# Less scratch for Pool, more tiles in four rings, and a norm moved to the end of a block in a hand-ordered attention and MLP kernel

## The chip, the cores and the metric

The kernel runs on one core of a Trainium2 chip. The metric is the device time of one execution in microseconds, from the start of the program to its end; lower is better.

## The reference

The layer takes x of 2048 rows by 512, computes an attention and a two-layer MLP from it, and mixes both by a gate for each row:

```python
q = (x @ wq).reshape(B, S, 32, 16).transpose(0, 2, 1, 3)
k, v = x @ wk, x @ wv                     # one head of 16 for all 32 query heads
p = softmax(einsum("bhqd,bkd->bhqk", q, k) * 16 ** -0.5)
a = einsum("bhqk,bkd->bhqd", p, v).transpose(0, 2, 1, 3).reshape(B, S, 512) @ wo
h = relu(x @ w1 + b1) ** 2                # 1792 hidden columns
b = h @ w2 + b2
g = sigmoid((x * gate_w).sum(-1, keepdims=True))
return g * a + (1 - g) * b
```

All inputs are float32, and the scores are large (wq and wk are scaled by about 36).

## The kernel before

Rows are worked on in four chunks of 512. Attention goes through 32 *groups* (a chunk and four heads; `it` counts them). A group is 32 *units*: a unit `u` is 128 keys by 256 queries for four heads. For each unit TensorE makes scores, ScalarE takes their exp into a tile `e` of 8 KB for each partition (two units share a tile), and TensorE multiplies the exps with v into `acc`. The second row of `acc` for each value holds the sums that the result is divided by.

A float32 product is made of three products of rounded halves: r and l, where r is the rounded value and l what is left. `split` makes both on VectorE. For weights `w_round` makes r on ScalarE or VectorE and `w_rest` makes l on VectorE. Other work has to be fitted in between: the query products (`q_unit`), the MLP (`hidden` for w1, `summed` for w2) and the output product (`projection`). They come as *spans* of up to 12 pairs of matmuls.

The order of the instructions is written out by hand: nothing is moved later. The main loop alternates two steps:

- `phase` scores some units ahead (`AHEAD` is 4) and places the pairs of a span between them, in an order that `PLANS` gives: M is a pair of the span, S0 the two halves of unit 0's scores in a PSUM tile `s` (two of these exist), and 02 and 12 the halves of unit 2, which go through the single PSUM bank `x` and are copied to `e` by VectorE (`score_copy`, L782).
- `context` multiplies the exps of 6 or 4 older units with v (L812). `block` chooses 6 or 4; a span of 12 is either put in one block of 6 units or halved over two blocks of 4.

While it writes the program, the planner keeps estimated clocks for three engines (`at_pe`, `at_act`, `at_dve`). `spend` fills VectorE's free time before a score copy is due, in this order: the l half of a rounded weight, `soon`, `divisions`, `chores`. A chore may be a load that is queued on SyncE; `held` then keeps the next chore back for some time (6 us by the plan).

`finish` ends a group. ScalarE copies `acc` out (L845), SyncE unpacks it into `oc` (values) and `lc` (sums) with two transfers (L203 and L204, called from `unpack`), and after each second group 24 small operations on VectorE divide (`divide`, L826 to L833); then Pool writes `oc` to the scratch array oTs (L859). When the first group of the next pair ends, a loop empties `divisions` before `oc` and `lc` are taken again. Later `ask` loads oTs into the stage tile (L961) and splits it into `orr` and `orl` (L191, L192) for the output product. `q_load` (L433) loads the queries of the next group with eight transfers.

`qnorm` makes the norms of the queries of a chunk: four small products into `x` (L412), two operations on VectorE (L347, L348), and writes on SyncE. It is called four times in the loop, at the start of a `phase`.

SyncE, ScalarE, VectorE and Pool work in the order of the program: a transfer that waits for its buffer holds all that are queued behind it on the same engine.

The pool `at` has these rings: e with 4 tiles, w1 pairs 3, w2 pairs 4, oc and lc one each. When the last query product is done, a fifth e tile is used as well, in the place of wql (`q_over`). By default 16384 bytes of each partition are set aside for the descriptors of Pool's transfers.

Of the kernel before, what the change touches and what calls it, by code (L numbers as in the profile page):

```python
# [10 lines left out]
F32 = mybir.dt.float32  # L11
# [21 lines left out]
ROOT = float(0x1fbd1df5 + 0x80000)  # L33
WARM = 10
PARTS = [slice(a, min(a + 86, CH)) for a in range(0, CH, 86)]
LANDS, DIVIDES = 6.0, 10.0
PAIR, CONTEXT, TURN, EXP, COPY, LATE = 0.235, 0.429, 0.36, 0.925, 0.66, 0.3
GROUPS = (0, 1, 2, 3), (4, 5, 6, 7), (8, 9, 10), (11, 12, 13)
AHEAD = 4
WHOLE, FIRST, SECOND = range(3)  # L40
PLANS = {
    (6, 12, WHOLE): ("M 02 S0 M S1 M M M M M S3 M M M S4 12 M M S5", (0, 1, 3, 4, 5, 2)),
    (6, 9, WHOLE): ("S0 M 03 M S1 M M M S2 M M M S4 13 M S5", (0, 1, 2, 4, 5, 3)),
    (6, 6, WHOLE): ("S0 M S1 M 03 M S2 M 13 M S4 M S5", (0, 1, 2, 4, 3, 5)),
    (6, 6, SECOND): ("S0 M S1 M 03 M S2 M 13 M S4 M S5", (0, 1, 2, 4, 3, 5)),
# [117 lines left out]
def mix_kernel(ctx: ExitStack, tc: tile.TileContext, xT, wkv, wq, wo, w12, b1, b2, cst, out):  # L163
# [63 lines left out]
    with fast, tc.tile_pool(name="at", bufs=1) as at, \  # L227
# [21 lines left out]
        def x_load(c):  # L249

            if c < 2:
                xw[c] = at.tile([128, KT, CH], F32, name="xf", tag="e", bufs=4)
                for a in range(2):
                    nc.sync.dma_start(xw[c][:, 2 * a:2 * a + 2], xT[c, 2 * a:2 * a + 2].rearrange("k p s -> p k s"))
            for k in range(KT):
                if c < 2:
                    xf[c, k] = xw[c][:, k]
                else:
                    xf[c, k] = at.tile([128, CH], F32, name="xk", tag="w2r" if c == 2 else "w2l", bufs=4)
                    nc.sync.dma_start(xf[c, k], xT[c, k])  # L260

        def wq_load(ts):
# [19 lines left out]

        kvp = [sp.tile([128, 2, CH], F32, name="s") for _ in range(2)]
        ks = {0: kvp[0][:, 0], 1: kvp[0][:, 1], 3: kvp[1][:, 0]}
        sqk = at.tile([96, NC, CH], BF, name="sqk", tag="e", bufs=4)
        kvc = at.tile([128, NC, CH], F32, name="kvc", tag="e", bufs=4)
        kvq, kb = {}, {}

        def kv_half(c, a):
# [153 lines left out]
                staged.append(keep.tile(sh, F32, name="stage", tag="r2"))  # L443
            return staged[0]

        room = [3, 4]
        at_pe, at_act, at_dve = 0.0, 0.0, 0.0

        def act(d, ready=0.0):
# [27 lines left out]
        def w_round(half, copy):  # L477
            n = len(rounded[half])
            assert n < room[half]
            rounded[half][n] = [at.tile([128, 512], F32R, name=f"w{half + 1}{x}", bufs=3 + half) for x in "rl"]  # L480
            copy(rounded[half][n][0], wf[half][n])
            if copy == scalar_copy:
                since[half][n] = act(0.64)
            else:
                since[half][n] = dve(0.46)

# [133 lines left out]
        def spend(until=None):  # L620

            nonlocal held

            def fits(d, ready=0.0):
                return until is None or max(at_dve, ready) + d <= until

            while True:
                due = [i for i in halves() if len(rounded[i]) > len(ws[i])]
                if due and fits(0.68, since[due[0]][len(ws[due[0]])]):
                    w_rest(due[0])  # L630
                elif soon and fits(soon[0][1]):
                    dve(soon[0][1])
                    soon.pop(0)[2]()
                elif divisions and fits(*divisions[0][:2]):
                    d, ready, f = divisions.pop(0)
                    dve(d, ready)
                    f()
                elif chores and fits(chores[0][0], held):
                    d, f = chores.pop(0)
                    dve(d, held if d else 0.0)  # L640
                    if f():
                        held = max(at_dve, at_pe) + 6.0
                else:
                    return

# [46 lines left out]
        def x_again(c):  # L692

            r, l = [xp.tile(sh, F32R, name=f"x{n}again{c}", tag=f"x{n}{c - 2}") for n in "rl"]
            def load(a):
                nc.sync.dma_start(stage()[:, :2], xT[c, 2 * a:2 * a + 2].rearrange("k p s -> p k s"))
                return True

            def part(k):
                split(r[:, k], l[:, k], stage()[:, k % 2])  # L700
                if k == KT - 1:
                    x[c] = r, l

# [36 lines left out]
            return (it, k // 2, k % 2) if it < NC * NG - 1 else (it, k % NK, k // NK)  # L740

        freed, used_x, made = [0.0, 0.0], [0.0], {}
        parts, copied, fifth = {}, {}, [None] * 4

        def e_half(u):

            for t in range(len(es), u // 2 + 1):
                if q_over and len(fifth) % 5 == 4:
                    es[t] = keep.tile([128, 4, CH], F32, name="e5", tag="r1")
                else:  # L750
                    es[t] = at.tile([128, 4, CH], F32, name="e", bufs=4)
                if q_over:
                    fifth.append(None)
            t = u // 2
            return es[t][:, :, u % 2 * HC:u % 2 * HC + HC]

# [44 lines left out]
        def context(acc, us):  # L801

            nonlocal at_pe
            at_pe += 0.12
            while us:
                u, (it, kt, q) = us[0], place(us[0])
                n = 2 if u % 2 == 0 and len(us) > 1 and it < NC * NG - 1 else 1
                at_pe = max([at_pe] + [made[i] + 0.06 for i in us[:n]]) + CONTEXT * n
                us = us[n:]
                cols, mine = slice(q * HC, (q + n) * HC), slice(u % 2 * HC, (u % 2 + n) * HC)  # L810
                for h in range(4):
                    nc.tensor.matmul(acc[h * 32:(h + 1) * 32, cols], v_ext[:, kt],  # L812
                                     es[u // 2][:, h % 2 * 2 + h // 2, mine], start=(kt == 0), stop=(kt == NK - 1),
                                     skip_group_check=True, tile_position=(0, h * 32))
            at_pe += 0.24

        ol = {}
# [17 lines left out]
        def finish(it, acc):  # L835
# [9 lines left out]
            nc.scalar.activation(a, acc, AF.Copy)  # L845
            act(0.62, at_pe)
            if u == 0:
                while divisions:
                    divisions.pop(0)[2]()
                ol[c, t] = [at.tile([128, CH], F32, name=n) for n in ("oc", "lc")]  # L850
            o, l = ol[c, t]
            unpack(nc.sync, o[u * 64:u * 64 + 64], l[u * 64:u * 64 + 64], a)
            if u == 1:
                for q, cols in enumerate(PARTS):
                    i = len(PARTS) * (4 * c + t) + q
                    divisions.extend((d, at_act + DIVIDES, f) for d, f in divide(o, l, cols, ok[:, i:i + 1]))
# [9 lines left out]
        def turn(a, u, js, okc, idle=0):  # L866

            if not o2:
                o2.append(at.tile([128, 4, 2, 4, DH], F32, name="o2", tag="oc"))
            js = slice(js[0], js[-1] + 1)  # L870
            m = js.stop - js.start
            if m > 2:
# [7 lines left out]
            n = at.tile([128, 2, 4, 4], F32, name="nl", bufs=2)[:, :, :m]  # L880
# [9 lines left out]
        def half(acc, q):  # L890

            js = range(2 * q, 2 * q + 2)
            a = at.tile([128, CH], F32, name="ah", tag="accs" if q else "lc")
            nc.vector.tensor_copy(a[:, :HC], acc[:, q * HC:q * HC + HC])
            busy(2 * q)
            if not q:
# [35 lines left out]
        def o_ready(c):  # L932

            if c == 0 and not wos:
                wos.extend(xp.tile(sh, F32R, name=n, tag=t) for n, t in (("wor", "xr2"), ("wol", "xl2")))

                def load(a):
                    nc.sync.dma_start(stage()[:, :2], wo[a * 256:a * 256 + 256].rearrange("(t p) n -> p t n", p=128))
                    return True

                for t in range(KT):
                    if t % 2 == 0:
# [5 lines left out]
        def ask(c, n=KT):  # L948
# [7 lines left out]
            def load(a):  # L956
# [2 lines left out]
                m = min(2, n - 2 * a)  # L959
                i = c * NG + 4 * a  # L960
                nc.sync.dma_start(stage()[:, :m], oTs[i:i + 2 * m].rearrange("(t u) d n -> (u d) t n", u=2))  # L961
                return True

            def part(t):
                orr, orl = tiles
# [9 lines left out]
        def ask_one(c, t):  # L975
# [5 lines left out]
            def load():  # L981
                i = c * NG + 2 * t
                nc.sync.dma_start(stage()[:, :1], oTs[i:i + 2].rearrange("(t u) d n -> (u d) t n", u=2))
                return True

            def part():
                split(osp[c][0][:, t], osp[c][1][:, t], stage()[:, 0])
# [141 lines left out]
        def phase(slots, n, m):  # L1129

            nonlocal scored, evicted, at_pe
            step_aside()
            if narrow:
                used_x[0] = dve(1.3) + 0.06
                qnorm(narrow.pop(0))
            if span.done[0] == 0:
                begin()
            kind = SECOND if span.done[0] else WHOLE if slots == span.slots else FIRST
            text, order = PLANS.get((n, slots, kind)) or plain(n, slots)
            rows = [], []  # L1140
            for item in text.split():
# [40 lines left out]
        def block(u):  # L1182
# [7 lines left out]
                return min(m, rest), left  # L1190
            if span.done[0] == 0 and left > 9:
                halved[0] += max(0.0, (total - 56 - u - 6 * units_left[0]) / (1.6 * max(units_left[0], 1)))
            if rest == 8 or rest == 4 or left > 9 and halved[0] >= 1.0 and rest != 6:
                halved[0] -= 1.0
                return 4, (left + 1) // 2
            return min(rest, 6), left

        halved, units_left = [0.5], [NC * (NF + 16) + 15 + 12]

        acc, us = None, ()  # L1200
        fetch()
# [79 lines left out]
```

## Time and profile before

| | us |
|---|---|
| median of 3 runs | 1242.66 |
| lowest and highest | 1241.65, 1244.49 |
| profiled execution, its own time | 1243.74 |
| its span, first to last instruction | 1242.0 |
| TensorE busy | 1219.7 |
| ScalarE busy | 1038.9 |
| VectorE busy | 767.0 |
| Pool busy | 67.3 |

The mean clock granted to TensorE is 0.992 of full speed. Busy times come from the one profiled execution, which took 1.08 us more than the median. In a row of the profile the engine stands first (PE is TensorE's matmuls, PEld its weight loads, DVE VectorE, ACT ScalarE, SP SyncE), then the line of the kernel and the tiles as out<-in. Matmul ends are modelled, so a busy PE may still be losing some tenths of a microsecond.

### The profile page before, as it was taken

What the parts mean: (1) busy time and instruction counts of PE and PEld (TensorE: products, weight loads), DVE (VectorE), ACT (ScalarE), POOL (GpSimd) and SP (SyncE); (2) the same over time, 40 slices, a digit from 0 to 9 for tenths busy, and PEclk for the clock granted to TensorE, in tenths of its full rate; (3) what the DMA queues carried; (4) which work ended last, traced back from release to release, by engine and by line L of the source; (5) the groups of instructions that cost most, each with busy time, mean ns of one, the idle gap of its engine ahead of it and who ended that gap; (6) DMA issues with size and microseconds to landing.
All of it is one profiled execution on the core that took longest, in us unless ns stands there. A gap on an engine that the chain in (4) does not pass through costs nothing.

```text
span 1242.0 us, 24097 instructions
## 1 busy us (share of the span) xinstructions
PE 1219.7 (98%) x9838; PEld 674.0 (54%) x9839; DVE 767.0 (62%) x1507; ACT 1038.9 (84%) x1151; POOL 67.3 (5%) x87
## 2 busy tenths in 40 slices
PE   9999999999999999999999999999999999999997
PEld 4554555555555545555555556555555555554553
DVE  6765667567485854738477674755838577465543
ACT  6788788888898878888798888888888888887864
POOL 1000120000000110000002001000000000000000
PEclk9999999999999999999999999999999999999989
DMA  6334331211213122102124212112112222300011
GB/s 225 85 106 112 91 94 42 65 57 56 64 61 116 56 82 94 58 21 65 56 82 132 77 41 92 46 48 65 62 67 61 73 65 82 90 31 27 23 51 37
DMA packets 45349, 88.72 MB, mean 71 GB/s; under 512 B 10643, under 2 KB 10899, under 8 KB 44721
## 3 DMA queue, kind: packets, MB, share of 16 engines
q1 hardware_dynamic: 37024, 68.27, 18.2%
q0 software_dynamic: 8064, 18.59, 4.7%
q8 instruction: 79, 1.29, 0.5%
q14 instruction: 38, 0.30, 0.1%
q10 hardware_dynamic: 144, 0.26, 0.1%
HBM read 57.83 MB, written 20.97 MB: 63 GB/s over the span
## 4 chain that ended last, share of the span: by engine, by line
PE 90%; ACT 5%; DVE 2%; DMA 1%; issue 1%; SPq 0%; ACTq 0%; DVEq 0%
PE acc L812 35%; PE mm L1102 31%; PE s L761 16%; PE x L761 5%; ACT e L798 4%; DMA stage<-oTs 1%; PE mm L295 0%; DMA qa<-qs 0%; DVE e L782 0%; PE acc L524 0%; PE mm L199 0%; DVE n L832 0%; ACT w1r L495 0%; DVE tmp L347 0%; SPq L433 0%
## 5 line engine op out<-in xcount | busy, mean ns | idle before, releaser
L798 ACT ACTIVATE e<-s 128x1024 f32<-128x1024 f32 x825 | 786.1, 1025 | 176.8 <-PE s L761 158.7
L812 PE MATMUL acc<-e,v_ext 128*32 128x512 f32 (+1 forms) x4224 | 487.4, 590 | 0.0
L782 DVE COPY e<-x 128x512 f32<-128x512 f32 x398 | 274.6, 690 | 329.2 <-PE x L761 284.5
L761 PE MATMUL s<-qa,k_aug 49*128 49x512 f32 x1650 | 466.4, 414 | 1.8 <-ACT e L798 1.2
L761 PEld LDWEIGHTS s<-qa,k_aug 49*128 49x128 f32 x1650 | 235.8, 185 | 79.5 <-ACT e L798 54.5
L812 PEld LDWEIGHTS acc<-e,v_ext 128*32 128x32 f32 x4224 | 117.2, 110 | 244.6 <-issue 241.3
L1102 PE MATMUL mm<-w2r,hr 64*128 64x512 f32 x896 | 228.5, 402 | 0.0
L798 ACT ACTIVATE e<-e 128x1024 f32<-128x1024 f32 x199 | 211.1, 1061 | 0.4 <-DVE e L782 0.4
L761 PE MATMUL x<-qa,k_aug 49*128 49x512 f32 x398 | 162.9, 409 | 7.8 <-DVE e L782 6.1
L1102 PEld LDWEIGHTS mm<-w2r,hr 64*128 64x128 f32 x896 | 136.0, 186 | 46.3 <-DVE hr L192 15.9
L1102 PE MATMUL mm<-w2l,hr 64*128 64x512 f32 x448 | 144.9, 393 | 0.0
L761 PEld LDWEIGHTS x<-qa,k_aug 49*128 49x128 f32 x398 | 74.3, 187 | 52.2 <-issue 10.9
L1102 PEld LDWEIGHTS mm<-w2l,hr 64*128 64x128 f32 x448 | 80.8, 186 | 6.8
L1102 PE MATMUL mm<-xragain,w1r 64*128 64x512 f32 x224 | 76.8, 418 | 0.2
L1102 PE MATMUL mm<-xr,w1r 64*128 64x512 f32 x224 | 74.1, 417 | 0.3
L1102 PE MATMUL mm<-xlagain,w1r 64*128 64x512 f32 x224 | 74.3, 391 | 0.0
L1102 PE MATMUL mm<-xragain,w1l 64*128 64x512 f32 x224 | 73.3, 392 | 0.0
L1102 PE MATMUL mm<-xl,w1r 64*128 64x512 f32 x224 | 72.4, 392 | 0.0
L1102 PE MATMUL mm<-xr,w1l 64*128 64x512 f32 x224 | 71.4, 393 | 0.0
L832 DVE RECIPROCAL n<-n 128x86 f32<-128x86 f32 x90 | 61.5, 684 | 2.0
L1102 PEld LDWEIGHTS mm<-xragain,w1r 64*128 64x128 f32 x224 | 38.4, 185 | 28.5 <-issue 11.7
L1102 PEld LDWEIGHTS mm<-xr,w1r 64*128 64x128 f32 x224 | 37.5, 185 | 27.5 <-issue 10.4
(162 smaller groups left out, 1178.2 us busy)
## 6 DMA issues: line engine op xcount, KB each, us to landing
stage<-in_w SPq DMA_DIRECT2D x56, 256.0 KB
qa<-qs SPq DMA_DIRECT2D x186, 64.0 KB
w1f<-in_w SPq DMA_DIRECT2D x28, 256.0 KB
w2f<-in_w SPq DMA_DIRECT2D x28, 256.0 KB
qs<-qr SPq DMA_DIRECT2D x16, 256.0 KB
ress<-res POOLq DMA_DIRECT2D x4, 1024.0 KB, 4.9
qs<-ql POOLq DMA_DIRECT2D x15, 256.0 KB, 8.7
oc<-accs SPq DMA_DIRECT2D x30, 128.0 KB
```

The source lines that it names most:

```text
L761: nc.tensor.matmul(dst.rearrange("p (a n) -> p a n", a=2), k_aug[rows, kt * 128:(kt + 1) * 128], qa[it][rows, :, q * HC:q * HC + HC], star ...
L782: nc.vector.tensor_copy(e_half(u)[:, 2 * r:2 * r + 2], x.rearrange("p (a n) -> p a n", a=2))
L798: nc.scalar.activation(e_half(u), src, AF.Exp, scale=SCALE)
L812: nc.tensor.matmul(acc[h * 32:(h + 1) * 32, cols], v_ext[:, kt], es[u // 2][:, h % 2 * 2 + h // 2, mine], start=(kt == 0), stop=(kt == NK ...
L832: return ((0.23, bound), (0.35, compare), (0.72, lambda: nc.vector.reciprocal(n[0], n[0])), (0.28, lambda: nc.vector.tensor_tensor(o[:, co ...
L1102: nc.tensor.matmul((self.before if r else self).bank, a[p], b[p], start=not r and i == 0, stop=r == 1 and i == len(self.terms[1]) - 1, ski ...
```

## The change

The diff makes these edits.

- Pool's descriptor scratch is 1024 bytes instead of 16384. The room goes to a fifth e tile (from the start of the kernel; the one in the place of wql becomes the sixth), a second oc and a second lc tile, and a fifth pair of w2 tiles (`room[1]` is 5).
- The loop that emptied `divisions` when the first group of a pair ends is gone.
- The l half of a weight that ScalarE rounds is planned 0.7 us later (`SURE`).
- A chore that loads returns its own hold: 6 us (`LANDS`) or, for the loads of `ask`, 10 us (`DIVIDES`). The division of the last chunk's third pair is planned 6 us after its copy instead of 10.
- `qnorm` is called at the end of `context` instead of the start of `phase`, and the planner counts its time on TensorE and VectorE. The block after it keeps its 12 slots together and uses the plan `LATER`, in which the first half of unit 2 comes behind S0, S1 and five pairs.
- `block` no longer halves a span when 10 units of a group are left.
- Smaller: the ring of `nl` has one tile, and the tiles that share the rings of oc and lc say bufs=2.

```diff
-LANDS, DIVIDES = 6.0, 10.0
+LANDS, DIVIDES, SURE = 6.0, 10.0, 0.7
-WHOLE, FIRST, SECOND = range(3)
+WHOLE, FIRST, SECOND, LATER = range(4)
 PLANS = {
     (6, 12, WHOLE): ("M 02 S0 M S1 M M M M M S3 M M M S4 12 M M S5", (0, 1, 3, 4, 5, 2)),
+    (6, 12, LATER): ("S0 M M S1 M M M 02 M S3 M M M S4 M 12 M M S5", (0, 1, 3, 4, 5, 2)),
...
-                xw[c] = at.tile([128, KT, CH], F32, name="xf", tag="e", bufs=4)
+                xw[c] = at.tile([128, KT, CH], F32, name="xf", tag="e", bufs=5)
...
-        room = [3, 4]
+        room = [3, 5]
...
-            rounded[half][n] = [at.tile([128, 512], F32R, name=f"w{half + 1}{x}", bufs=3 + half) for x in "rl"]
+            rounded[half][n] = [at.tile([128, 512], F32R, name=f"w{half + 1}{x}", bufs=3 + 2 * half) for x in "rl"]
             copy(rounded[half][n][0], wf[half][n])
             if copy == scalar_copy:
-                since[half][n] = act(0.64)
+                since[half][n] = act(0.64) + SURE
...
                     dve(d, held if d else 0.0)
-                    if f():
-                        held = max(at_dve, at_pe) + 6.0
+                    wait = f()
+                    if wait:
+                        held = max(at_dve, at_pe) + wait
...
-        parts, copied, fifth = {}, {}, [None] * 4
+        parts, copied, sixth = {}, {}, [None] * 5
...
-                if q_over and len(fifth) % 5 == 4:
+                if q_over and len(sixth) % 6 == 5:
                     es[t] = keep.tile([128, 4, CH], F32, name="e5", tag="r1")
                 else:
-                    es[t] = at.tile([128, 4, CH], F32, name="e", bufs=4)
+                    es[t] = at.tile([128, 4, CH], F32, name="e", bufs=5)
...
                                      skip_group_check=True, tile_position=(0, h * 32))
+            if narrow:
+                at_pe = max(at_pe + 0.2, used_x[0] + 0.05)
+                qnorm(narrow.pop(0))
+                late.append(True)
+                used_x[0] = dve(1.3, at_pe + 0.2) + 0.06
             at_pe += 0.24
...
             if u == 0:
-                while divisions:
-                    divisions.pop(0)[2]()
-                ol[c, t] = [at.tile([128, CH], F32, name=n) for n in ("oc", "lc")]
+                ol[c, t] = [at.tile([128, CH], F32, name=n, bufs=2) for n in ("oc", "lc")]
...
-                    divisions.extend((d, at_act + DIVIDES, f) for d, f in divide(o, l, cols, ok[:, i:i + 1]))
+                    divisions.extend((d, at_act + (LANDS if (c, t) == (NC - 1, 2) else DIVIDES), f) for d, f in divide(o, l, cols, ok[:, i:i + 1]))
...
                 nc.sync.dma_start(stage()[:, :m], oTs[i:i + 2 * m].rearrange("(t u) d n -> (u d) t n", u=2))
-                return True
+                return DIVIDES
...
             step_aside()
-            if narrow:
-                used_x[0] = dve(1.3) + 0.06
-                qnorm(narrow.pop(0))
             if span.done[0] == 0:
                 begin()
             kind = SECOND if span.done[0] else WHOLE if slots == span.slots else FIRST
+            if late and (n, slots, kind) == (6, 12, WHOLE):
+                kind = LATER
+            late.clear()
...
-            if rest == 8 or rest == 4 or left > 9 and halved[0] >= 1.0 and rest != 6:
+            if rest == 8 or rest == 4 or left > 9 and halved[0] >= 1.0 and rest not in (6, 10) and not late:
...
-    nc = bacc.Bacc("TRN2", target_bir_lowering=False, num_devices=1)
+    nc = bacc.Bacc("TRN2", target_bir_lowering=False, num_devices=1, dynamic_dma_scratch_size=1024)
```

The lines left out set bufs=5 for the other users of the ring e, bufs=5 for the tiles of x in the rings of w2, `LANDS` as the hold of the other loads, and the ring sizes of nl, o2 and ah.

More of the change, by code (lines that the diff above doesn't have):

```diff
@@ L258, in x_load @@
                 else:
-                    xf[c, k] = at.tile([128, CH], F32, name="xk", tag="w2r" if c == 2 else "w2l", bufs=4)
+                    xf[c, k] = at.tile([128, CH], F32, name="xk", tag="w2r" if c == 2 else "w2l", bufs=5)
                     nc.sync.dma_start(xf[c, k], xT[c, k])
@@ L284, in mix_kernel @@
         ks = {0: kvp[0][:, 0], 1: kvp[0][:, 1], 3: kvp[1][:, 0]}
-        sqk = at.tile([96, NC, CH], BF, name="sqk", tag="e", bufs=4)
-        kvc = at.tile([128, NC, CH], F32, name="kvc", tag="e", bufs=4)
+        sqk = at.tile([96, NC, CH], BF, name="sqk", tag="e", bufs=5)
+        kvc = at.tile([128, NC, CH], F32, name="kvc", tag="e", bufs=5)
         kvq, kb = {}, {}
@@ L696, in load @@
                 nc.sync.dma_start(stage()[:, :2], xT[c, 2 * a:2 * a + 2].rearrange("k p s -> p k s"))
-                return True
+                return LANDS
             def part(k):
@@ L742, in mix_kernel @@
         freed, used_x, made = [0.0, 0.0], [0.0], {}
-        parts, copied, fifth = {}, {}, [None] * 4
+        parts, copied, sixth = {}, {}, [None] * 5
         def e_half(u):
             for t in range(len(es), u // 2 + 1):
-                if q_over and len(fifth) % 5 == 4:
+                if q_over and len(sixth) % 6 == 5:
                     es[t] = keep.tile([128, 4, CH], F32, name="e5", tag="r1")
                 else:
-                    es[t] = at.tile([128, 4, CH], F32, name="e", bufs=4)
+                    es[t] = at.tile([128, 4, CH], F32, name="e", bufs=5)
                 if q_over:
-                    fifth.append(None)
+                    sixth.append(None)
             t = u // 2
@@ L868, in turn @@
             if not o2:
-                o2.append(at.tile([128, 4, 2, 4, DH], F32, name="o2", tag="oc"))
+                o2.append(at.tile([128, 4, 2, 4, DH], F32, name="o2", tag="oc", bufs=2))
             js = slice(js[0], js[-1] + 1)
@@ L879, in turn @@
             l = p5[:, :, :, 0, 1]
-            n = at.tile([128, 2, 4, 4], F32, name="nl", bufs=2)[:, :, :m]
+            n = at.tile([128, 2, 4, 4], F32, name="nl")[:, :, :m]
             nc.vector.tensor_scalar(n[:, 0], l, L_MIN, L_MAX, op0=OP.max, op1=OP.min)
@@ L892, in half @@
             js = range(2 * q, 2 * q + 2)
-            a = at.tile([128, CH], F32, name="ah", tag="accs" if q else "lc")
+            a = at.tile([128, CH], F32, name="ah", tag="accs" if q else "lc", bufs=1 if q else 2)
             nc.vector.tensor_copy(a[:, :HC], acc[:, q * HC:q * HC + HC])
@@ L938, in load @@
                     nc.sync.dma_start(stage()[:, :2], wo[a * 256:a * 256 + 256].rearrange("(t p) n -> p t n", p=128))
-                    return True
+                    return LANDS
                 for t in range(KT):
@@ L961, in load @@
                 nc.sync.dma_start(stage()[:, :m], oTs[i:i + 2 * m].rearrange("(t u) d n -> (u d) t n", u=2))
-                return True
+                return DIVIDES
             def part(t):
@@ L983, in load @@
                 nc.sync.dma_start(stage()[:, :1], oTs[i:i + 2].rearrange("(t u) d n -> (u d) t n", u=2))
-                return True
+                return LANDS
             def part():
@@ L1196, in block @@
             return min(rest, 6), left
-        halved, units_left = [0.5], [NC * (NF + 16) + 15 + 12]
+        late, halved, units_left = [], [0.5], [NC * (NF + 16) + 15 + 12]
         acc, us = None, ()
```

## The prediction

> **What bounds the kernel now.** I read the page first, then a table of busy time by stage, then the stretches in which TensorE stood still.
>
> ```profile
> span 1242.0 us, 24097 instructions
> ...
> PE 1219.7 (98%) x9838; PEld 674.0 (54%) x9839; DVE 767.0 (62%) x1507; ACT 1038.9 (84%) x1151; POOL 67.3 (5%) x87
> ```
>
> TensorE is busy for 98% of the span. A change that leaves the products as they are can only win stretches in which TensorE waits or runs slowly. The table by stage says where these lie; its first columns are the stretch, its length and PE's busy time.
>
> ```profile
> 36.10:165.00 128.90, 124.77 (x1003) 65.24 (x1003) 81.36 (x151) 102.11 (x113) 11.18 (x16) 1.00 0.36 94
> 165.00:440.00 275.00, 274.60 (x2250) 154.17 (x2251) 184.30 (x358) 241.16 (x269) 15.30 (x11) 1.00 0.22 66
> 440.00:1190.00 750.00, 744.37 (x6044) 414.74 (x6042) 458.97 (x910) 645.09 (x711) 36.05 (x47) 0.99 0.21 66
> 1190.00:1242.00 52.00, 41.76 (x393) 22.78 (x390) 19.20 (x47) 27.85 (x31) 0.00 (x0) 0.90 0.06 23
> ```
>
> From 165 to 440 us PE loses 0.40 us in 275: there is nothing to win there. It loses 128.90 - 124.77 = 4.13 us in the stage of the query products (36 to 165), 5.63 us from 440 to 1190, and 10.24 us in the tail. The middle stage also has a clock of 0.99, and PE's own timeline shows why. The bracket is PE's idle time before the row, with what ended it.
>
> ```profile
> 459.82 0.61 PE L761 MATMUL x<-qa,k_aug 49*128 49x512 f32 x1 [2.19 <-DVE e L782]
> 598.73 0.50 PE L761 MATMUL x<-qa,k_aug 49*128 49x512 f32 x1 [1.37 <-DVE e L782]
> 1124.63 0.50 PE L761 MATMUL x<-qa,k_aug 49*128 49x512 f32 x1 [1.67 <-DVE e L782]
> ```
>
> Three times the second score copy of a block waits for the first: the bank x is single, and VectorE had not emptied it. That is 2.19 + 1.37 + 1.67 = 5.23 us of the stage's 5.63. Right behind each of them the granted clock (the column after the count) is half.
>
> ```profile
> 460.06:463.46 3.40, 3.40 (x19) 0.50 0.01 2
> 600.00:603.40 3.40, 3.40 (x18) 0.50 0.31 111
> 1125.66:1129.06 3.40, 3.40 (x18) 0.50 0.02 5
> 1197.33:1204.15 6.82, 6.82 (x44) 0.50 0.00 0
> ```
>
> PE counts as busy there but does half the work, so 3.40 / 2 = 1.70 us are lost in each of the first three, 5.10 together. The three stalls cost 10.33 us, twice what the idle column says. The fourth, in the tail, follows the transposes of the last groups, which the change leaves alone.
>
> [...]
>
> **The change part by part.** First the three stalls and who made VectorE late.
>
> ```profile
> 458.01 0.43 DVE L191 CAST orr<-stage 128x512 fp32r<-128x512 f32 x1 [4.95 <-DMA stage<-oTs]
> 1122.82 0.43 DVE L191 CAST orr<-stage 128x512 fp32r<-128x512 f32 x1 [4.15 <-DMA stage<-oTs]
> ```
>
> ```profile
> 594.15 0.61 DVE n L832
> ...
> 597.83 0.24 DVE oc L833
> 598.07 0.61 DVE e L782
> ```
>
> ```profile
> 447.32 0.48 SPq L203 DMA_DIRECT2D oc<-accs  x1
> 448.54 4.71 SPq L433 DMA_DIRECT2D qa<-qs  x8
> 454.45 0.39 SPq L961 DMA_DIRECT2D stage<-oTs  x1
> ```
>
> ```profile
> 444.79 2.39 DMA oTs<-oc
> ```
>
> *Stalls at 460 and 1124.* VectorE stands in the split of an attention chunk, whose load SyncE issued late: at 454.45 it came behind eight query loads (4.71 us), and these behind L203, which waited until the single oc buffer had been written out (444.79 + 2.39 = 447.18). Two edits meet here. With two oc and lc buffers L203 no longer waits for that write, so the query loads go ahead of 447; the stage load still needs the write, and could start near 447.2. And `ask` now holds its splits 10 us after a load is queued, not 6. The waits were 4.95 and 4.15 us: 4 us more leaves 0.95 and 0.15, less than the 1.37 that hurt. I take both stalls as gone.
>
> *Stall at 599.* The chain runs through divisions from 594.15 to 598.07 without a break: 3.92 us of the loop that empties `divisions` when the first group of the next pair ends. The change deletes the loop; the second buffer makes that safe, and each division waits for a gap. I take the stall as gone.
>
> So 5.23 + 5.10 = 10.33 us off. If only the 4 us of hold worked and the freed divisions landed before some other score copy, the third would stay (1.37 + 1.70 = 3.07), which leaves 7.26.
>
> *Cover of the longer hold.* Two loads for each chunk, 4 us later each: 8 us. The split at 1122.82 is first used at 1174.46, so 51 us hide 8. If that cover were gone, blocks would run without products; the price is below.
>
> ```profile
> 1174.46 0.39 PE L1102 MATMUL mm<-wor,orr 64*128 64x512 f32 x1
> ```
>
> *Fifth exp tile, and the moved norms.* Six units in a block and four scored ahead make ten units, or five tiles; the early stage has four. So ScalarE waits in the middle of a block until the context product has read the oldest tile.
>
> ```profile
> ACT e L798 <- PE acc L812: 17.8, 10, 2.4
> PEld x L761 <- DVE tmp L347: 2.7, 4, 0.7
> PE x L761 <- DVE tmp L347: 1.5, 4, 0.4
> ```
>
> ```profile
> 106.24 2.78 PE L812 MATMUL acc<-e,v_ext 128*32 128x512 f32 x24
> 114.60 1.92 PE L812 MATMUL acc<-e,v_ext 128*32 128x512 f32 x16
> ...
> 350.64 2.78 PE L812 MATMUL acc<-e,v_ext 128*32 128x512 f32 x24
> 357.78 2.78 PE L812 MATMUL acc<-e,v_ext 128*32 128x512 f32 x24
> ```
>
> All ten waits lie before the extra tile that the kernel already has comes into use. Block to block the early one takes 114.60 - 106.24 = 8.36 us, the later one 7.14: up to 1.22 us each, 12.2 for ten. Many blocks lose less, and the stage's idle time is only 4.13 us, in which the norms' 1.5 us (four times) stand too. The norm keeps its place on PE, behind the context product; new is the LATER order, which puts the first score copy behind three others, so PE no longer stands before a bank that VectorE is still reading. I take 4.13 us for tile and norms together, with ends 1.5 and 12.2. The norm's four small SyncE writes now come ahead of the next group's query load: 4 x 4.71 / 8 = 2.4 us later for something that is used a group later (32 units at 7.14 us for six, 38 us), so nothing. The sixth tile later on lies behind five that suffice: nothing.
>
> *Held splits.* The low half of a weight now waits 0.7 us longer in the plan for ScalarE's rounding.
>
> ```profile
> DVE w2l L490 <- ACT w2r L495: 49.0, 25, 3.1
> ```
>
> These waits stand where PE lost nothing (0.40 us from 165 to 440), so I take zero; its ends are the 0.7 us of a score copy pushed back and one stall saved (3.4).
>
> *Fifth w2 pair.* It frees the planner to round earlier. Zero, if ScalarE has room; otherwise the first slower rival.
>
> *Scratch.* Pool's transfers lose ring space.
>
> ```profile
> qs<-ql POOLq DMA_DIRECT2D x15, 256.0 KB, 8.7
> ```
>
> Fifteen in the stage of 128.9 us, one each 8.6 us, landing after 8.7: hardly more than one is in flight. Were each to wait for the one before, Pool would start some of them a little late, and Pool has 5% to do. Zero. [...] The other buffer edits (nl, ah, o2) and the order six-four in place of four-six move nothing on PE.
>
> *New stalls.* Nearly every VectorE slot moves. Between 165 and 1190 us the trace has three such stalls, each 10.33 / 3 = 3.44 us, and each is a chance meeting of queues. I charge one, with ends 0 and four (13.8).
>
> *Sum*, on the profiled run's 1243.74 us (span 1242.0, 1.74 around it): 1243.74 - 10.33 - 4.13 + 3.44 = 1232.7. The median of the runs is 1.08 us lower, so 1231.6.
>
> **The rivals.**
>
> *A: the gate still closes.* If residual waits near 1.4 us remain at the three places, idle time shrinks but the half-speed windows stay, and 5.10 us come back: 1236.7. For it: 1.37 us was enough once. Against: the residues above are under 1 us. Chance 0.12.
>
> *B: new stalls eat it.* Four instead of one, 10.3 us more: 1241.9, no difference. 0.08.
>
> *C, slower: ScalarE takes the w2 roundings.*
>
> ```profile
> L798 ACT ACTIVATE e<-s 128x1024 f32<-128x1024 f32 x825 | 786.1, 1025 | 176.8 <-PE s L761 158.7 <-PE acc L812 17.8
> L495 ACT ACTIVATE w2r<-w2f 128x512 fp32r<-128x512 f32 x14 | 8.8, 629 | 0.0
> L481 DVE CAST w2r<-stage 128x512 fp32r<-128x512 f32 x15 | 6.3, 420 | 0.0
> L481 DVE CAST w2r<-w2f 128x512 fp32r<-128x512 f32 x14 | 5.9, 419 | 0.0
> ```
>
> VectorE now rounds 15 + 14 = 29 of the w2 tiles. With a fifth pair the planner may see room to give all to ScalarE: 29 x 0.629 = 18.2 us. A block's six exps take 6 x 1.025 = 6.15 us of 7.14, so one rounding fits and a second does not; from that point each delays the next scores. If all fell so: 1231.6 + 18.2 = 1249.8. Against it: ScalarE idles 176.8 us before exps. 0.12.
>
> *D, slower: projections arrive late.* If the hold leaves blocks without products, such a block lasts the exps' 6.15 us. Its PE work is 7.14 less twelve of eighteen steps at (7.14 - 2.78) / 18 = 0.24, so 4.23: 1.9 us lost each. Eight of them, two for each chunk, give 1246.8. It decides when the 8 us exceed the lead; the one lead read above is 51. 0.08.
>
> *That the buffers do not act* would leave the holds and the LATER order alone; it lies inside A.
>
> **How the numbers follow.** Forecast 0.60, A 0.12, B 0.08, C 0.12, D 0.08. The time is the forecast's, 1231.6. Its own range runs from the high end of the early stage without a charge (1243.74 - 10.33 - 12.2 - 1.08 = 1220.1) to the third stall staying and one more new one (1231.6 + 3.07 + 3.44 = 1238.1). The whole range, 1222 to 1247, takes in A, B and D and leaves out most of C and the last of the fast end. About 0.2%, 2.5 us, is what a measurement can tell from no change: forecast and A are faster (0.72), B the same (0.08), C and D slower (0.20).
>
> **What would show it.** Right: from 440 to 1190 PE idle falls from 5.6 us to about 2 and the half-clock windows from three to one at most; the wait of ScalarE's exp for acc disappears; no score copy follows a run of divisions; L203 no longer waits for oTs. Wrong: ScalarE's w2r count rises by 20 or more while PE waits for exps; projections start late; or new half-clock windows stand elsewhere. If Pool's writes land far later than 8.7 us and something waits for them, I misjudged the scratch.

## The result, and the profile after

| | before | after |
|---|---|---|
| median of 6 runs each, us | 1243.31 | 1228.05 |
| lowest to highest, us | 1241.65 to 1247.31 | 1223.29 to 1231.57 |
| profiled execution, its own time, us | 1243.74 | 1228.71 |
| its span, us | 1242.0 | 1227.0 |

The ratio is 0.9873 (95% interval 0.985 to 0.9896): 15.3 us off, where 11.1 were forecast. The page first:

```profile
span 1227.0 us, 24104 instructions
...
PE 1211.2 (99%) x9839; PEld 673.4 (55%) x9839; DVE 771.2 (63%) x1516; ACT 1035.5 (84%) x1146; POOL 66.3 (5%) x87
```

The work is the same and so are the busy times, within 1% (Pool's 1.5%); what went is time in which TensorE stood or ran slowly. The table by stage, after:

```profile
36.10:165.00 128.90, 127.74 (x1062) 69.78 (x1060) 87.03 (x161) 106.38 (x117) 11.28 (x16) 1.00 0.38 99
165.00:440.00 275.00, 271.18 (x2204) 152.07 (x2206) 185.40 (x366) 234.89 (x261) 16.08 (x12) 0.99 0.22 69
440.00:1175.00 735.00, 734.74 (x6008) 410.53 (x6000) 454.31 (x899) 639.42 (x705) 34.20 (x46) 1.00 0.22 65
1175.00:1227.00 52.00, 43.65 (x431) 23.70 (x430) 21.27 (x48) 31.88 (x35) 0.00 (x0) 0.97 0.06 22
```

The same two last stretches of the kernel before, for comparison:

```profile
440.00:1175.00 735.00, 729.37 (x5925) 407.10 (x5923) 451.17 (x894) 632.20 (x698) 34.98 (x45) 0.99 0.21 65
1175.00:1242.00 67.00, 56.76 (x512) 30.42 (x509) 27.00 (x62) 40.73 (x44) 1.07 (x2) 0.92 0.11 41
```

PE's idle time from 440 to 1175 falls from 5.63 to 0.26 us, and its clock there rises from 0.99 to 1.00. The counts of matmuls (x, behind PE's busy time) say the same in work: 83 more in that stretch, 59 more (1062 against 1003) from 36 to 165. One stage got worse: 165 to 440 lost 0.40 us before and loses 3.82 now, with a clock of 0.99. The timelines of PE, VectorE and SyncE there, and the clock behind the stall:

```profile
170.37 0.79 PE L763 MATMUL x<-qa,k_aug 49*128 49x512 f32 x1 [3.44 <-DVE e L784]
```

```profile
168.56 0.43 DVE L192 CAST wor<-stage 128x512 fp32r<-128x512 f32 x1 [5.34 <-DMA stage<-in_wo]
```

```profile
156.59 6.68 SPq L420 DMA_DIRECT2D qs<-nrm  x4
163.31 0.45 SPq L943 DMA_DIRECT2D stage<-in_wo  x1
```

```profile
168.80:175.50 6.70, 5.13 (x21) 1.43 (x21) 5.95 (x10) 1.97 (x2) 6.09 (x4) 0.50 0.32 83
```

It is the old stall in a new place. SyncE needs 6.68 us for the four writes of the norm, so the load of wo starts at 163.31; its split is held back 6 us by the plan and VectorE stands 5.34 us for it; the second score copy of that block comes late; and the clock is half behind it. The two other waits that the prediction wanted gone are gone. ScalarE's exp no longer waits for acc (besides the row below it has 0.8 us of waits for a score copy), and SyncE's transfer into oc waits for the copy of acc alone, no longer for oTs. That transfer is L203 in the kernel before, which the second row is of, and L204 in the changed one:

```profile
ACT e L800 <- PE s L763: 165.3, 197, 4.6
```

```profile
SPq L203 <- DMA oTs<-oc: 102.0, 12, 24.5
```

```profile
SPq L204 <- ACT accs L852: 245.3, 30, 30.9
```

### The profile page after: what moved, and what is told of

Same layout as the page of the kernel before. It is cut to its first block, busy times and chain, and to the rows that moved or that the text cites. A ratio compares the mean times of both kernels' runs of the same rounds, so it can differ in the third digit from the quotient of the medians.

```text
span 1227.0 us, 24104 instructions
## 1 busy us (share of the span) xinstructions
PE 1211.2 (99%) x9839; PEld 673.4 (55%) x9839; DVE 771.2 (63%) x1516; ACT 1035.5 (84%) x1146; POOL 66.3 (5%) x87
## 3 DMA queue, kind: packets, MB, share of 16 engines
q8 instruction: 79, 1.29, 0.5%
## 4 chain that ended last, share of the span: by engine, by line
PE 93%; DVE 2%; ACT 2%; DMA 1%; SPq 1%; issue 1%; DVEq 0%; ACTq 0%
PE acc L814 37%; PE mm L1107 33%; PE s L763 17%; PE x L763 6%; ACT e L800 1%; DVE e L784 1%; SPq L420 1%; DMA stage<-in_wo 0%; DMA xf<-in_xT 0%; PE mm L296 0%; PE mm L200 0%; DVE qr L392 0%; DVE ql L393 0%; PE s L306 0%; DVE ot L1249 0%
## 5 line engine op out<-in xcount | busy, mean ns | idle before, releaser
L784 DVE COPY e<-x 128x512 f32<-128x512 f32 x404 | 279.1, 691 | 389.1 <-PE x L763 354.1
L800 ACT ACTIVATE e<-e 128x1024 f32<-128x1024 f32 x202 | 214.7, 1063 | 0.8 <-DVE e L784 0.8
```

The source lines that it names most:

```text
L784: nc.vector.tensor_copy(e_half(u)[:, 2 * r:2 * r + 2], x.rearrange("p (a n) -> p a n", a=2))
L800: nc.scalar.activation(e_half(u), src, AF.Exp, scale=SCALE)
```

## The experiments

The theory was the prediction's: the stalls are meetings of SyncE's queue with VectorE's order, each named edit removes those at its place, and the terms add. The main rival: any new order of VectorE's work removes old stalls and makes new ones. The runs of the kernel before that stood beside them had medians of 1242.14 to 1242.90 us.

### Parts of the change put into the kernel before

**The scratch alone.**

```diff
+    nc = bacc.Bacc("TRN2", target_bir_lowering=False, num_devices=1, dynamic_dma_scratch_size=1024)
```

> The kernel before with Pool's descriptor scratch at 1024 bytes and nothing else. Theory (the scratch costs nothing, the room is what counts): same as before, 1243.3 within 2.5 us, the query writes by Pool still land after 7 to 9 us, and the three stalls and half-clock windows stand where they stood (460, 600, 1126 us). Rival (ring space matters): Pool's issues stretch, its writes land 2 us or more later, and the time moves by more than 2.5 us.

1241.7 us, ratio 0.9989 (0.9974 to 1.0004): no difference. Pool's query writes landed after 7.6 us in this run. The room is free here. One thing came out otherwise than the theory said: all three stalls were there, but only the first (2.39 us long) had its half-speed window. The two others did not, as PE's timeline and the clock right behind them show.

```profile
604.36 0.50 PE L761 MATMUL x<-qa,k_aug 49*128 49x512 f32 x1 [1.38 <-DVE e L782]
...
1128.93 0.50 PE L761 MATMUL x<-qa,k_aug 49*128 49x512 f32 x1 [1.78 <-DVE e L782]
```

```profile
604.60:608.00 3.40, 3.40 (x29) 1.42 (x29) 1.35 (x2) 2.31 (x3) 0.05 (x1) 1.00 0.29 112
...
1128.90:1132.30 3.40, 3.37 (x27) 1.44 (x29) 1.97 (x4) 2.00 (x3) 0.00 (x0) 1.00 0.02 5
```

**Two oc tiles, no emptying loop, and the longer hold.**

```diff
-                while divisions:
-                    divisions.pop(0)[2]()
+                ol[c, t] = [at.tile([128, CH], F32, name=n, bufs=2) for n in ("oc", "lc")]
...
-                return True
+                return DIVIDES
```

> The kernel before with the small scratch, two oc and lc tiles, the emptying loop deleted, and the 10 us hold of ask. Theory (three chance meetings of queues, 10.3 us with their half-clock windows): 1233 us, PE idle from 440 to 1190 us falls from 5.6 to under 1.5, and no half-clock window is left there. Rival (any new order of VectorE's work removes old stalls and makes new ones): the time moves by less than 4 us either way, and other half-clock windows stand between 165 and 1190. Rival (the exp tile brings the gain): under 2 us here.

1228.89 us, ratio 0.9887 (0.9868 to 0.9906): 13.6 us off. By stage:

```profile
165.00:440.00 275.00, 274.56 (x2250) 153.63 (x2248) 185.84 (x358) 241.18 (x268) 15.24 (x12) 1.00 0.21 66
440.00:1175.00 735.00, 734.71 (x6010) 411.22 (x6008) 456.32 (x907) 640.91 (x706) 34.09 (x46) 1.00 0.21 67
1175.00:1226.50 51.50, 43.16 (x430) 23.54 (x426) 21.48 (x50) 31.49 (x34) 0.00 (x0) 0.99 0.08 27
```

The stage from 440 lost 0.29 us of PE time instead of 5.63, no half-speed window was left in it, and no new stall appeared. The rival expected new ones; this edit made none.

**Each of the two alone.** First the buffers without the hold:

```diff
-                while divisions:
-                    divisions.pop(0)[2]()
-                ol[c, t] = [at.tile([128, CH], F32, name=n) for n in ("oc", "lc")]
+                ol[c, t] = [at.tile([128, CH], F32, name=n, bufs=2) for n in ("oc", "lc")]
```

> The kernel before with the small scratch, two oc and lc tiles and the emptying loop deleted, and the old 6 us hold. Theory: the stall at 600 goes (3.1 us with its window), the one at 460 goes or shrinks because L203 no longer waits (up to 3.9 us), the one at 1124 stays: 1236 to 1239. Rival (the hold alone does the work): same as before within 2.5 us. Rival (the buffers alone do it): 1229.

1234.9 us, ratio 0.9944 (0.9924 to 0.9964). VectorE's only wait for a stage load is now the late one:

```profile
1116.87 0.43 DVE L191 CAST orr<-stage 128x512 fp32r<-128x512 f32 x1 [4.44 <-DMA stage<-oTs]
```

Then the hold without the buffers:

```diff
-                        held = max(at_dve, at_pe) + 6.0
+                        held = max(at_dve, at_pe) + wait
...
                 nc.sync.dma_start(stage()[:, :m], oTs[i:i + 2 * m].rearrange("(t u) d n -> (u d) t n", u=2))
-                return True
+                return DIVIDES
```

> The kernel before with the 10 us hold of ask's loads and nothing else (one oc, the emptying loop stays). Theory: VectorE's waits of 4.95 and 4.15 us for the stage load shrink below 1 us, so the stalls at 460 and 1124 go with their windows, 7.3 us; the stall at 600 stays: 1235. Rival (the buffers do the work at 460): only the stall at 1124 goes, 3.4 us: 1239.

1233.64 us, ratio 0.992 (0.9899 to 0.994). One score-copy stall of this size is left, the one behind the emptying loop:

```profile
599.86 0.50 PE L762 MATMUL x<-qa,k_aug 49*128 49x512 f32 x1 [1.39 <-DVE e L783]
```

It too has the full clock behind it:

```profile
600.50:603.90 3.40, 3.40 (x31) 1.51 (x30) 1.46 (x3) 2.72 (x3) 0.00 (x0) 1.00 0.37 139
```

So the stall at 1124 belongs to the hold, the one at 599 to the loop, and either edit removes the one at 460. That is why 7.5 and 9.3 us, 16.8 together, give 13.6: the stall at 460, 2.19 + 1.70 = 3.9 us, is in both.

**One exp tile more.**

```diff
-                    es[t] = at.tile([128, 4, CH], F32, name="e", bufs=4)
+                    es[t] = at.tile([128, 4, CH], F32, name="e", bufs=5)
```

> The kernel before with the small scratch and one exp tile more (five, later six). Theory: ScalarE's ten waits for the context product go, and 2.5 to 4 us of the query stage with them, so about 1240 us; the three later stalls stay. Rival (the exp tile is the main part): 1233 us or less. Rival (ScalarE's waits cost nothing): same within 2.5 us.

1238.43 us, ratio 0.9973 (0.9947 to 0.9998): 4.1 us off. The query stage holds 1038 matmuls instead of 1003 and PE idles 2.16 us in it instead of 4.13; ScalarE's waits for acc were gone, and the three later stalls stayed. The runs spread from 1232.67 to 1249.79 us, and the interval only just leaves out 1.

```profile
36.10:165.00 128.90, 126.74 (x1038) 68.56 (x1038) 83.21 (x154) 104.68 (x116) 11.31 (x16) 1.00 0.38 96
```

**The norms alone**, with LATER and the rule of halving.

```diff
+            if narrow:
+                at_pe = max(at_pe + 0.2, used_x[0] + 0.05)
+                qnorm(narrow.pop(0))
...
-            if narrow:
-                used_x[0] = dve(1.3) + 0.06
-                qnorm(narrow.pop(0))
...
-            if rest == 8 or rest == 4 or left > 9 and halved[0] >= 1.0 and rest != 6:
+            if rest == 8 or rest == 4 or left > 9 and halved[0] >= 1.0 and rest not in (6, 10) and not late:
```

> The kernel before with the norms called at the end of context, the plan LATER and the changed rule of halving; no new room. Theory: PE's waits for the norm's VectorE work (1.5 us, four times) go, 1.5 us off, so 1241.8; the three later stalls may shift, since the division into blocks changes. Rival (replanning alone decides): more than 4 us either way with stalls in new places.

1252.28 us, ratio 1.0073 (1.0056 to 1.009): 9.8 us slower. Here the rival was right. VectorE's timeline has waits for loads that the kernel before did not have (for wo it had 0.9 us), and behind four of these stand half-speed windows. The second is the wait for wo that the changed kernel has too; without the norm edit (below) there is none, so that stall came with this edit. The other half of the rival holds as well: PE's stalls at 460 and 599 are gone in this profile, though no edit meant for them is in it.

```profile
90.38 0.43 DVE L482 CAST w1r<-w1f 128x512 fp32r<-128x512 f32 x1 [4.82 <-DMA w1f<-in_w]
...
175.35 0.43 DVE L192 CAST wor<-stage 128x512 fp32r<-128x512 f32 x1 [4.38 <-DMA stage<-in_wo]
...
264.79 0.43 DVE L482 CAST w2r<-stage 128x512 fp32r<-128x512 f32 x1 [1.49 <-DMA stage<-in_w]
...
1021.71 0.43 DVE L482 CAST w2r<-stage 128x512 fp32r<-128x512 f32 x1 [1.71 <-DMA stage<-in_w]
```

```profile
93.10:96.50 3.40, 3.40 (x20) 0.64 (x14) 2.08 (x4) 1.93 (x2) 0.69 (x1) 0.50 0.27 57
178.50:181.90 3.40, 3.40 (x20) 1.65 (x20) 2.18 (x4) 2.65 (x4) 3.40 (x3) 0.51 0.47 159
267.20:270.60 3.40, 3.40 (x17) 0.59 (x16) 1.65 (x3) 1.97 (x2) 0.00 (x0) 0.50 0.60 187
1025.00:1028.40 3.40, 3.40 (x20) 0.87 (x16) 2.98 (x6) 2.25 (x3) 0.00 (x0) 0.50 0.01 2
```

Counted in the trace's timeline of the context products, the blocks of six units fall from 106 to 100 and those of four rise from 94 to 103.

### Parts taken out of the changed kernel

**The norms back in their old place**, everything else as changed (the diff above, read backwards).

> The changed kernel with the norms back at the start of phase, without LATER and with the old rule of halving; everything else of the change stays. Theory (parts add: the norm edit is a loss, as alone, and the two oc tiles with the hold and the exp tile carry the gain): before less 13.6 less 4.1, about 1225, so 3 us faster than the changed kernel, with the blocks divided as before and no VectorE wait for a load. Rival (the norm edit costs only where w2 is short of a pair, and wins 2 us here): 1230.

1225.3 us, ratio to before 0.9858 (0.984 to 0.9876). The sum of the parts said 1225. That reads as "the norm edit loses 3 us", but the next run corrects it. The query stage of this kernel, for that comparison:

```profile
36.10:165.00 128.90, 126.69 (x1039) 68.88 (x1039) 84.12 (x156) 105.43 (x118) 11.24 (x16) 1.00 0.40 104
```

**The splits of wo held 14 us.**

```diff
-                    return LANDS
+                    return 14.0
```

> The changed kernel with one number changed: the splits of wo are held 14 us behind their load, not 6. Theory (the new stall at 165 to 175 us is the same meeting of SyncE and VectorE, 5.3 us of VectorE waiting): the stall and its half-clock window go, 4.6 + 1.7 = 6.3 us less in a run that has it, so 1222 to 1224 and a narrower spread. Rival (the stall moves to the next load): within 2.5 us of the changed kernel's 1228.

1222.30 us (1221.39 to 1226.63), ratio to before 0.9841 (0.9819 to 0.9862). The stage with the new stall is clean:

```profile
36.10:165.00 128.90, 127.80 (x1060) 69.93 (x1059) 87.05 (x161) 106.37 (x117) 11.28 (x16) 1.00 0.41 105
165.00:440.00 275.00, 274.61 (x2256) 154.47 (x2252) 190.54 (x376) 239.49 (x265) 17.42 (x15) 1.00 0.22 68
```

Its median is 5.8 us below the changed kernel's, close to what the stall cost in its profile: 3.44 us of idle time and half of the 5.13 us that PE was busy in the slow window, 6.0. The intervals of the two ratios overlap a little (0.9819 to 0.9862 against 0.985 to 0.9896), and they were not timed side by side, so "faster than the changed kernel" is likely and not shown. It is 3 us below the kernel without the norm edit. With its stall cured, that edit gains about what its stage shows: 1060 matmuls instead of 1039, and 21 x 128.90 / 1060 = 2.6 us (an estimate, since matmuls differ in length: in the changed kernel those into `acc` took 586 ns on the mean, those into `s` 413).

**Four w2 pairs.**

```diff
-        room = [3, 5]
+        room = [3, 4]
```

> The changed kernel with four w2 pairs again (room 4). Theory (the norm edit divides the blocks differently, and with four pairs VectorE must round w2 tiles whose load was just queued): waits of VectorE for w2 loads come back as in the norm edit alone, two to four of them with half-clock windows, so 1235 to 1241. Rival (the fifth pair does nothing): same as the changed kernel within 2.5 us. Rival (the fifth pair crowds ScalarE): faster than the changed kernel.

1239.75 us, ratio to before 0.9968 (0.9951 to 0.9985): 11.7 us worse than with five. VectorE's waits for w2 loads are back, of the same tiles and about as long as in the norm edit alone. Between 165 and 1175 us PE idles 4.7 us more than in the changed kernel, and two more half-speed windows (from 257.79, 6.83 us long, and from 1015.55, 3.41) cost 5.1; that is 9.8 of the 11.7.

```profile
256.97 0.43 DVE L482 CAST w2r<-stage 128x512 fp32r<-128x512 f32 x1 [1.56 <-DMA stage<-in_w]
...
1012.79 0.43 DVE L482 CAST w2r<-stage 128x512 fp32r<-128x512 f32 x1 [1.65 <-DMA stage<-in_w]
```

### Parts taken out of the kernel with the longer hold for wo

**Four exp tiles.**

```diff
-                    es[t] = at.tile([128, 4, CH], F32, name="e", bufs=5)
+                    es[t] = at.tile([128, 4, CH], F32, name="e", bufs=4)
```

> The kernel of the longer hold for wo (1222.3 us) with one exp tile less (four, later five). Theory: ScalarE's waits for the context product come back in the query stage, and with them the 3.9 us that the exp tile alone saved there: 1226. Rival (with the norms in their new place the early stage has slack): within 2.5 us of 1222.

1226.92 us, ratio to before 0.9868 (0.9848 to 0.9889): 4.6 us worse than with the tile by the medians, though the intervals of the two ratios overlap a little. ScalarE waits for the context product again:

```profile
ACT e L800 <- PE acc L814: 17.0, 9, 2.4
```

**No slack for the rounding.**

```diff
-                since[half][n] = act(0.64) + SURE
+                since[half][n] = act(0.64)
```

> The kernel of the longer hold for wo (1222.3 us) with the 0.7 us for ScalarE's rounding taken back. Theory (these waits of VectorE stand where TensorE loses nothing): same as that kernel, 1222 within 2.5 us, with VectorE's waits for w2r near 2.1 us each again. Rival (they delay score copies): slower by one stall or more, 1226 or above.

1223.61 us, ratio to before 0.9837 (0.9814 to 0.9861): no difference, although the waits of w1l and w2l for ScalarE's rounding, 0.4 us in all with the slack, are back:

```profile
DVE w2l L491 <- ACT w2r L496: 43.3, 26, 2.1
DVE w1l L491 <- ACT w1r L496: 12.3, 25, 2.1
```

**The old rule of halving.**

```diff
-            if rest == 8 or rest == 4 or left > 9 and halved[0] >= 1.0 and rest not in (6, 10) and not late:
+            if rest == 8 or rest == 4 or left > 9 and halved[0] >= 1.0 and rest != 6 and not late:
```

> The kernel of the longer hold for wo (1222.3 us) with the old rule that a span may be halved when 10 units of a group are left; the norms stay where they are. Theory (the rule of halving, not the norms, changed the division into blocks): the profile shows 106 blocks of six again instead of 100, and new meetings of queues cost one or two stalls, 1225 to 1229. Rival (the norms' whole block changed the division): 100 blocks of six stay, same time within 2.5 us.

1222.93 us, ratio to before 0.9832 (0.9807 to 0.9857): no difference. The profile has 106 blocks of six and 94 of four again, so the rule did change the division; by itself that costs nothing once the waits are out of the way. The plan `LATER` and the earlier division of the last chunk's third pair were not tried by themselves.

## Why the prediction was right, and where it was not

**The three stalls (10.33 us).** Right in place and cause, and the edits named for them take 13.6 us. VectorE's waits at 460 and 1124, of which 0.95 and 0.15 us were to remain, are gone. The 3.3 us more are about what the fourth half-speed window cost (6.82 / 2), which the prediction left standing as untouched; this is read from two profiled executions. PE's idle time before the product behind those transposes is the same in both kernels (before, then two oc tiles with the hold), yet only the first has a half-speed window behind it (for the other, the clock of 0.99 over 51.50 us above leaves no room for one of 6.82):

```profile
1195.94 0.49 PE L1102 MATMUL mm<-wor,orr 64*128 64x512 f32 x1 [1.29 <-DVE peek L1125]
```

```profile
1185.31 0.49 PE L1101 MATMUL mm<-wor,orr 64*128 64x512 f32 x1 [1.29 <-DVE peek L1124]
```

What took that window away is not shown: of the seven profiles with this stall of 1.29 us, three have a window behind it (the kernel before, the scratch alone, the buffers alone) and four do not. That it went was luck for the forecast. The same holds for the stalls at 599 and 1124: 1.37 and 1.67 us of idle time were followed by half speed in the kernel before, 1.38, 1.39 and 1.78 us in others were not. Taking each window as a sure 1.70 us was too firm for stalls of 1.37 to 1.78 us.

**How the stall at 460 goes.** Here a step failed: "the query loads go ahead of 447". With two oc tiles L203 still went out at 446.58 (SyncE's timeline of the kernel with the buffers alone); what it waits for there is ScalarE's copy of acc. The stall went in both single runs all the same: with the buffers alone the stage load started at 452.55 instead of 454.45 and VectorE no longer waited for it.

```profile
446.58 0.47 SPq L203 DMA_DIRECT2D oc<-accs  x1
...
452.55 0.39 SPq L959 DMA_DIRECT2D stage<-oTs  x1
```

Those 1.9 us are the smaller part. It is VectorE's order that moved. In the kernel before, the divisions end at 444.49, the last split of the load before runs at 446.68, and VectorE is at the next split at 453.06 and stands there until 458.01. With the buffers alone the divisions run until 449.79 and both splits come later, the second of them 10.6 us behind its load. VectorE's timelines, before and then with the buffers alone:

```profile
446.68 0.41 DVE L191 CAST orr<-stage 128x512 fp32r<-128x512 f32 x1
```

```profile
451.38 0.42 DVE L191 CAST orr<-stage 128x512 fp32r<-128x512 f32 x1
...
463.14 0.42 DVE L191 CAST orr<-stage 128x512 fp32r<-128x512 f32 x1
```

**Fifth exp tile and norms (4.13 us).** The tile alone gives 4.1 us, and 4.6 in the cleaned kernel. The norms were wrongly read as an edit of their own stage. There they work: PE idles 1.16 us in it after the change, 2.16 with the tile alone. But the edit alone was 9.8 us slower, because it reorders all that follows. (`LATER` puts the first score copy behind two scores, S0 and S1, not three.) The size was too small as well. The prediction took the stage's idle time, 4.13 us, for tile and norms together; by the runs they give 4.1 + 3.0 = 7.1 (the 3.0 in the kernel with the longer hold). The stage says the same in matmuls: 59 more, and 59 x 128.90 / 1062 = 7.2 us (an estimate again), while PE's idle time in it fell by only 2.97. The idle column did not show all that there was to win.

**Fifth w2 pair (zero) and rival C.** The largest mis-sized term: beside the norm edit the pair is worth 11.7 us, since with four VectorE rounds tiles whose load was just queued. Without the norm edit zero was right as far as the runs show: the kernel that has the pair and not the norms gains 17.1 us, and the parts without the pair, 13.6 + 4.1, make 17.7. The prediction looked for its price on ScalarE. That did not come: of 56 w2 tiles ScalarE rounded 56 - 29 = 27 before, and after the change 15 + 11 = 26.

```profile
L496 ACT ACTIVATE w2r<-stage 128x512 fp32r<-128x512 f32 x15 | 9.5, 631 | 0.0
...
L496 ACT ACTIVATE w2r<-w2f 128x512 fp32r<-128x512 f32 x11 | 7.0, 633 | 0.0
```

**The order of six and four.** "Move nothing on PE" was wrong for the division into blocks and right for the time, as far as the run with the old rule shows it.

**New stalls (3.44 us).** One was charged and one came, but it cost 6.0 us in the profiled run: PE stood 3.44 us, where the three old ones had 1.74 each on average, and its half-speed window was twice as long (6.70 us). The count is luck: the norm edit alone made four with half-speed windows, the two oc tiles with the hold none. And the place could have been seen. The prediction had the norm's four writes on SyncE take 2.4 us and delay nothing but a query load, so it put them at nothing. In the kernel before, the last four took 4.88 us (from 161.13), with the load of wo right behind them at 166.06. In the changed kernel they took 6.68 us, the load of wo again stood behind them, and VectorE waited for it.

**Held splits, scratch, cover of the hold.** Zero each, as forecast; no projection came late (rival D), and rivals A and B did not decide. D's cover was read at its longest. At 460 the last split of the kernel before, at 459.68, is first used at 465.2, 5.5 us later and not 51; with the longer hold the projection there starts later (468.5, with two oc tiles) and PE does not stand for it.

The sum was 4.2 us short of the change measured. By the medians of these runs the three stalls' edits gave 3.3 us more than forecast, tile and norms 3.0 more, and the new stall took 5.8 instead of 3.44, 2.4 more; 0.6 is lost where the parts do not add (17.1 against 17.7). That makes 3.3. The other 0.9 is the difference between the two medians of the kernel before, 1243.31 here and 1242.39 to 1242.50 beside these parts. So the time lies near the forecast partly because errors of 2 to 3 us, each hardly larger than what the runs can tell apart, went against each other.

## What to carry to other kernels

In a hand-ordered kernel with a nearly full TensorE, read the few stalls of a microsecond or two one by one: here all but one were a load queued late on one engine and an instruction for it placed early on another (the one was a run of divisions ahead of a score copy), and one more buffer or 4 to 8 us more of hold removed them. Price an edit that reorders the rest by the slack it uses up elsewhere, not by its own stage: the norms' move lost 9.8 us alone and won about 3 with a fifth w2 pair and a longer hold. Try the parts alone and taken out, since two that cure the same stall do not add.

## What the runs showed of the hardware

Idle times of TensorE of 1.29 to 1.39 us were followed by a half-speed window in two of the five cases shown (1.37 us, with the window from 600.00, and 1.29 us, with the one from 1197.33, both in the kernel before) and not in the others (1.38 us with the scratch alone, 1.39 with the hold alone, 1.29 with two oc tiles and the hold). The 1.78 us with the scratch alone passed at full clock too. So in these profiles the length of an idle time does not tell by itself whether half speed follows; what else decides is not shown.

The start of the program varies as well: the kernel before ran from 25.9 to 39.6 us at full clock in its profile, the one with the small scratch alone at half, and got 56 matmuls done there instead of 98. Why is not shown: PE's timeline of the profile with the small scratch lists no wait from 22 to 40 us.

```profile
25.90:39.60 13.70, 13.49 (x98) 8.65 (x97) 11.92 (x24) 10.18 (x11) 0.90 (x1) 1.00 0.35 111
```

```profile
25.90:39.60 13.70, 13.70 (x56) 10.96 (x55) 8.84 (x19) 8.63 (x9) 0.00 (x0) 0.50 0.33 106
```

This goes with the spread between runs of one kernel (for the small scratch 1239.8 us at a mean granted clock of 0.995 to 1246.4 at 0.988), and it bounds what a single profile can tell of a term of a few microseconds.
